# A transformer block on one core: v's weights loaded before q's and k's, five narrower loads for q and k, v's product first on the tensor engine, a new written-out order

## Chip, cores and metric

The kernel runs on one core of a Trainium2 chip. The metric is device time in microseconds (us). The kernel before took 241.88 us, the median of 3 runs (241.85 to 241.88). Engines are named as in the profile: PE is the tensor engine (PEld its weight loads), DVE the vector engine, ACT the scalar engine, POOL GpSimd, SP the engine whose queue issues nearly all DMAs.

## What is computed

One block for 2048 tokens of width 448 (bf16): a sliding, dilated attention (16 heads of 28; each token sees 8 keys, 2 apart), then a gated feed-forward layer whose gate mixes tokens by a 2048x2048 matrix.

```python
def _A_ref(x, wqkv, wo):                      # wqkv: 448 x 1344, columns q | k | v
    qkv = (x @ wqkv) ...                      # 3 x 16 heads x 2048 x 28
    idx = pos[:, None] - 2 * arange(8)        # keys of a token
    attn = softmax(einsum(q, k[idx]) * 28**-0.5, masked where idx < 0)
    return (attn @ v[idx]) @ wo
def _B_ref(x, w_in, w_sp, b_sp, w_out):
    z = gelu(x @ w_in)                        # 2048 x 1792
    z1, z2 = z[:, :896], layernorm(z[:, 896:])
    g = w_sp @ z2 + b_sp[:, None]             # 2048 x 2048 matrix
    return (z1 * g) @ w_out
h = x + _A_ref(layernorm(x), A_wqkv, A_wo)
out = h + _B_ref(layernorm(h), ...)
```

## The kernel before, in words

**Tiling.** Tokens lie in 16 tiles of 128. `x_tm` holds x by token; DVE takes mean and variance of each tile (L614 `bn_stats`, L616), POOL the reciprocal root (L608, L609), DVE writes the normalised tile `xn` (L625). The 448 columns are laid out as four chunks that start at 0, 128, 192 and 320, so that a product over 448 is made of three full 128-row chunks and one half of a fourth: chunk 1 (rows 128 to 255) and chunk 2 (rows 192 to 319) overlap by 64 rows, and a product reads all of one and the other half of the other. Tiles 0 to 3 are transposed by PE against the identity (L654, four 128x128 products each) and copied out of PSUM into `xhT` by ACT or DVE (jobs `xe0` to `xe3`, L512); tiles 4 to 15 are transposed by DMA on SP's queue (L526).

**Products.** `product` (L496) issues every large product as full matmuls (F: 128 rows) and half matmuls (H: 64 rows, two side by side in the array's upper and lower half). `qk{t}_{g}` makes q and k for token range t (0 to 255, 256 to 511, then 512 each) and head group g; its weights `wqk` are copied from the raw load `wraw` into a padded layout (jobs `wp`, L512, on ACT and DVE). `v0`, `v2`, ... make v for two blocks of keys each, with weights `wv` that are read as loaded. The logits are L790, exp is ACT's L799, the mask DVE's L805, the weighted sum L814, the output projection `y` L496 again. The feed-forward half is z2 and z1 (L496), the token-mixing product (L951; in groups of four matmuls, 16 per PSUM bank), the add of b_sp by DVE (L960, reads `bb`) which frees the bank, the gate (L963), and the last product (L975), add (L982) and store.

**Order.** The code makes a list of 920 jobs, each for one engine, with what it reads and writes. A written-out list of numbers, `ORDER`, is the one order in which all jobs are issued (919 is a dummy matmul, `warm`, L990, put in while PE has nothing to do); `BANK` names the PSUM bank of each product; `ON` the engine of each copy. Each engine runs its jobs in that order and waits on semaphores, so a job that waits holds up all behind it on its engine. SP's queue is such an engine: a transfer's turn comes when those ahead of it are issued. Loads at the start are called in the order of `FIRST` (L530 ff.), but `ORDER` decides.

Which chunks of `wraw` a product of q or k reads is set by `WK` (full matmuls) and by `(3, 1)` in `qk`'s half matmuls.

Of the kernel before, what the change touches and what calls it, by code (L numbers as in the profile page):

```python
# [76 lines left out]
ON = {'xe0_0': 'act', 'xe1_0': 'act', 'wp3_0': 'act', 'wp2_0': 'act', 'xe0_1': 'dve', 'wp1_0': 'dve', 'wp2_1': 'dve',  # L77
# [3 lines left out]
    'act', 'qe3_3': 'dve', 'od0': 'pool', 'od1': 'pool', 'qe2_1': 'act', 've6': 'act', 'qe3_0': 'dve', 'od3': 'pool',  # L81
    'od2': 'pool', 'qe3_2': 'act', 've8': 'dve', 'od4': 'dve', 'od6': 'pool', 'qe3_1': 'act', 'qe4_1': 'act', 'qe4_0':
    'act', 'od5': 'pool', 'qe4_2': 'act', 'qe4_3': 'act', 've10': 'act', 'od7': 'dve', 'od8': 'dve', 'od9': 'dve',
    've14': 'act', 've16': 'act', 've12': 'act', 'od11': 'pool', 'od10': 'pool', 'oc11': 'dve', 'z2c1': 'act', 'z2c3':
    'act', 'z2c2': 'dve', 'od12': 'pool', 'od13': 'pool', 'oc12': 'act', 'oc13': 'act', 'od15': 'dve', 'od14': 'pool',
    'z2c4': 'act', 'od17': 'pool', 'oc14': 'act', 'oc15': 'act', 'od16': 'dve', 'oc17': 'dve', 'z2c6': 'act', 'z2c7':
    'act', 'z2c5': 'act', 'oc16': 'dve', 'z2c9': 'act', 'z2c8': 'act', 'z2c10': 'act', 'z2c13': 'act'}
# [960 lines left out]
```

## Time and profile before

| | us |
|---|---|
| median of 3 runs | 241.88 |
| the profiled execution: its time | 242.38 |
| its span, first to last instruction | 240.7 |
| PE busy | 233.6 |
| DVE / ACT / POOL busy | 148.9 / 93.6 / 32.3 |
| first product that is not `warm` or a transposition | at 9.99 |
| last product ends | at 237.86 |

Times in the text are from the start of the span. The page gives busy time of each engine, the span in 40 slices, the DMA queues, the chain of work that ended last, and groups of instructions. The views behind it give single instructions in order of time with the idle time ahead of each and what ended it. In such a row the first number is the start, the second the length, `x4` the count, and the bracket the wait. TensorE's granted clock is 1.0 over the whole span.

### The profile page before, as it was taken

The page shows a single profiled execution, that of the slowest core. Times are in us where ns is not written, and L with a number is a line of the kernel's source. Part 1 is how long each engine was busy: PE and PEld are TensorE (multiplying, and loading weights), DVE is VectorE, ACT ScalarE, POOL GpSimd, SP SyncE. Part 2 cuts the span into 40 slices and gives each one's busy share as a digit, 9 for nine tenths or more (in the row PEclk, how much of TensorE's full clock was granted, in tenths as well). Part 3 has the DMA queues.
Part 4 walks back from the last instruction along what each step waited for, and adds up shares of the span by engine and source line. Part 5 has one row for each costly group of instructions (what it writes and reads, how often), then busy time and mean ns, then how long its engine had stood idle before and what let it go on. Part 6 is the DMA issues. An engine that isn't in the chain of part 4 may idle for free.

```text
span 240.7 us, 4205 instructions
## 1 busy us (share of the span) xinstructions
PE 233.6 (97%) x1711; PEld 114.9 (48%) x1727; DVE 148.9 (62%) x319; ACT 93.6 (39%) x115; POOL 32.3 (13%) x75
## 2 busy tenths in 40 slices
PE   7799999999999999999999999999999999999995
PEld 4565445445555444444444444444444444444462
DVE  5898977899999776877965037311506214317453
ACT  2577858799698978786820000000000000000000
POOL 6442000005331213114060000000000000000000
PEclk9999999999999999999999999999999999999999
DMA  6944244378947536499999997000000000110012
GB/s 174 364 107 99 48 85 85 84 180 213 127 94 83 102 75 132 87 121 191 198 194 175 152 189 184 3 0 0 0 0 3 20 19 0 57 60 0 0 57 95
DMA packets 66393, 23.21 MB, mean 96 GB/s; under 512 B 58694, under 2 KB 66246, under 8 KB 66374
## 3 DMA queue, kind: packets, MB, share of 16 engines
q1 hardware_dynamic: 66304, 22.95, 45.9%
q8 instruction: 13, 0.21, 0.4%
q14 instruction: 6, 0.05, 0.1%
q10 hardware_dynamic: 70, 0.00, 0.0%
HBM read 6.84 MB, written 1.84 MB: 36 GB/s over the span
## 4 chain that ended last, share of the span: by engine, by line
PE 93%; DMA 3%; DVE 1%; SPq 1%; issue 1%
PE psum L496 39%; PE psum L951 39%; PE psum L975 9%; PE psum L814 3%; PE psum L790 3%; DMA wraw<-in_A_wqkv_dram 3%; SPq L527 1%; DVE ub L960 1%; DVE z1p L963 0%; DVE srg L982 0%; DVE wqk L512 0%
## 5 line engine op out<-in xcount | busy, mean ns | idle before, releaser
L960 DVE TENSOR_TENSOR ub<-psum,bb 128x512 bf16<-128x512 f32 x28 | 19.2, 690 | 54.5 <-PE psum L951 54.1
L951 PE MATMUL psum<-wsp_hi,z2p 128*128 128x512 bf16 x219 | 49.9, 379 | 0.3
L951 PEld LDWEIGHTS psum<-wsp_hi,z2p 128*128 128x128 bf16 x224 | 21.9, 98 | 26.1
L799 ACT ACTIVATE E<-psum 128x896 bf16<-128x896 f32 (+2 forms) x36 | 31.8, 927 | 5.7 <-PE psum L790 5.7
L496 PE MATMUL psum<-xhT,wqk 128*128 128x512 bf16 (+3 forms) x154 | 26.5, 335 | 1.7 <-DVE wqk L512 0.9
L951 PE MATMUL psum<-wsp_lb,z2p 128*128 128x512 bf16 x111 | 25.6, 379 | 0.1
L951 PE MATMUL psum<-wsp_la,z2p 128*128 128x512 bf16 x108 | 24.9, 379 | 0.2
L496 PE MATMUL psum<-w_in,hnT 128*128 128x448 bf16 (+1 forms) x128 | 24.7, 353 | 0.0
L496 PE MATMUL psum<-hnT,w_in 128*128 128x512 bf16 (+1 forms) x112 | 23.9, 379 | 0.0
L975 PE MATMUL psum<-w_out,z1p 128*128 128x448 bf16 (+1 forms) x119 | 22.5, 341 | 0.0
L614 DVE BATCH_NORM_STATS2 st<-x_tm 128x6 f32<-128x448 bf16 x32 | 19.3, 613 | 2.0 <-DMA x_tm<-in_A_x_dram 2.0
L805 DVE TENSOR_TENSOR E<-E,maskb 128x1792 bf16<-128x1792 bf16 (+2 forms) x18 | 19.6, 1101 | 1.1 <-ACT E L799 1.1
L877 DVE BATCH_NORM_STATS2 st<-z2p 128x6 f32<-128x448 bf16 x32 | 18.6, 607 | 1.4 <-ACT z2p L873 1.2
L982 DVE TENSOR_TENSOR srg<-psum,x_tm 128x448 bf16<-128x448 f32 (+1 forms) x17 | 9.6, 592 | 13.7 <-PE psum L975 13.7
L496 PEld LDWEIGHTS psum<-xhT,wqk 128*128 128x128 bf16 (+1 forms) x160 | 12.1, 97 | 11.7 <-issue 2.8
L951 PEld LDWEIGHTS psum<-wsp_lb,z2p 128*128 128x128 bf16 x112 | 11.0, 98 | 13.2
L951 PEld LDWEIGHTS psum<-wsp_la,z2p 128*128 128x128 bf16 x112 | 10.9, 98 | 13.2
L609 POOL TENSOR_TENSOR rs<-rs,negh 128x2 f32<-128x2 f32 (+2 forms) x22 | 16.7, 759 | 1.8
L975 PEld LDWEIGHTS psum<-w_out,z1p 128*128 128x128 bf16 x119 | 11.6, 98 | 10.0
L496 PEld LDWEIGHTS psum<-w_in,hnT 128*128 128x128 bf16 (+1 forms) x128 | 10.2, 97 | 11.7 <-issue 2.6
L512 ACT ACTIVATE qkT<-psum 128x1024 bf16<-128x1024 f32 (+1 forms) x17 | 13.6, 825 | 3.3 <-PE psum L496 3.0
L496 PEld LDWEIGHTS psum<-hnT,w_in 128*128 128x128 bf16 (+1 forms) x112 | 8.9, 97 | 12.2 <-issue 2.8
(54 smaller groups left out, 226.3 us busy)
## 6 DMA issues: line engine op xcount, KB each, us to landing
w_in<-in_B_w_in_dram SPq DMA_DIRECT2D x8, 224.0 KB, 3.6
out_dram<-srg SPq DMA_DIRECT2D x16, 112.0 KB, 1.7
x_tm<-in_A_x_dram SPq DMA_DIRECT2D x3, 448.0 KB, 7.3
w_out<-in_B_w_out_dram SPq DMA_DIRECT2D x1, 784.0 KB, 5.1
bb<-in_B_b_sp_dram SPq DMA_DIRECT2D x1, 512.0 KB, 6.2
wraw<-in_A_wqkv_dram SPq DMA_DIRECT2D x1, 448.0 KB, 6.4
wraw<-in_A_wqkv_dram SPq DMA_DIRECT2D x2, 224.0 KB, 6.4
wv<-in_A_wqkv_dram SPq DMA_DIRECT2D x2, 224.0 KB, 6.4
```

The lines of the kernel that those rows point to most:

```text
L496: ins = e.matmul(o, w, x, start=g not in seen, stop=left[g] == 0, **kw)
L512: j = pl.job(name, eng, key, [(lambda e: e.activation(o(), i(), AF.Copy) if eng == "act" else e.tensor_copy(o(), i()), list(reads), list(w ...
L609: (lambda e: e.tensor_tensor(R, A, negh[:, 0:1].to_broadcast([128, n]), ALU.pow), [rr, r_negh], r_rs[k][m:m + n])],
L614: [(lambda e: e.bn_stats(st[:, m, :], src), [rsrc], [r_st[k][m]])], dve_t(D))
L790: ins = e.matmul(psum[:, c:c + nq], qkT[p:p + DH, 2 * g + 1, k0:k0 + NK], qkT[p:p + DH, 2 * g, t0:t0 + nq], start=True, stop=True, tile_po ...
L799: return e.activation(o, i, AF.Exp, scale=SCALE)
L805: return e.tensor_tensor(a, a, maskb[:, 0:1, pad:pad + nq].to_broadcast([NK, NHEAD, nq]), ALU.mult)
L877: [(lambda e, m=m, k=k: e.bn_stats(st3[:, m, k, :], z2p[:, m, D * k:D * (k + 1)]), [r_z2[m]], [r_st[2][m]])], dve_t(D))
L951: ins = e.matmul(psv(tk), z2p[:, s, 128 * fc:128 * fc + 128], w[:, 512 * (tc % 2):512 * (tc % 2) + 512], start=(s == 0), stop=(s == NB - 1))
L960: [(lambda e, tc=tc, s=s, tk=tk: e.tensor_tensor(ub[:, s, :], psv(tk), bb[:, 512 * tc:512 * tc + 512], ALU.add), [r_bb], [r_ub[s]])], dve_ ...
L975: ins = e.matmul(psv(tk, 0, c1 - c0), z1p[:, fc, 128 * m:128 * m + 128], w_out[:, fc, c0:c1], start=(fc == 0), stop=(fc == FC7 - 1))
L982: [(lambda e, m=m, s=s, tk=tk, c0=c0, c1=c1: e.tensor_tensor(srg[:, s, c0:c1], psv(tk, 0, c1 - c0), x_tm[:, m, c0:c1], ALU.add), [r_x[m]], ...
```

## The change

1. **Loads of q's and k's weights.** Before: three transfers, chunk 0, chunks 1 and 2, chunk 3, each with q's and k's columns (448 KB the largest, 896 KB in all). After: five transfers, 784 KB: chunks 0 and 1 of the new layout (rows 0 to 127 and 320 to 447; q and k, 448 KB), rows 192 to 319 for q alone (112 KB), rows 256 to 319 for k (64 partitions, 56 KB), rows 128 to 191 for q (64 partitions, 56 KB), rows 128 to 255 for k (112 KB). The half matmuls of k now read chunk 2 of `wraw`, the full ones of q chunks 0, 1 and 2, of k chunks 0, 1 and 3. Rows that no product reads are not loaded.
2. **Copies into `wqk`.** Those of k take two chunks instead of three (`wp{g}_1`); the odd rows are three copies instead of two (`wp4_0`, `wp4_1`, `wp4_2`).
3. **A new `ORDER`, `BANK` and `ON`**, for the whole kernel.

On SP's queue, the first transfers before (in the program's order; `wraw` is q and k, `wv` is v, `x_tm` x):

```order
L527 DMA x_tm<-in_A_x_dram 128x448 x2
L527 DMA x_tm<-in_A_x_dram 128x2x448
L527 DMA x_tm<-in_A_x_dram 128x4x448
L527 DMA wraw<-in_A_wqkv_dram 128x2x896
L527 DMA wraw<-in_A_wqkv_dram 128x896 x2
L527 DMA x_tm<-in_A_x_dram 128x4x448
L527 DMA wo<-in_A_wo_dram 64x448
L527 DMA wv<-in_A_wqkv_dram 128x2x448
```

and after (the two of 64 partitions are k's rows 256 to 319, then q's rows 128 to 191; the last two are k's chunk 3, then q's chunk 2):

```order
L530 DMA x_tm<-in_A_x_dram 128x448 x2
L530 DMA x_tm<-in_A_x_dram 128x2x448
L530 DMA wv<-in_A_wqkv_dram 128x2x448 x2
L530 DMA x_tm<-in_A_x_dram 128x4x448
L530 DMA wraw<-in_A_wqkv_dram 64x448 x2
L530 DMA wraw<-in_A_wqkv_dram 128x2x896
L530 DMA wraw<-in_A_wqkv_dram 128x448 x2
L530 DMA x_tm<-in_A_x_dram 128x4x448
```

Both transfers of v's weights have moved from places 10 and 14 to places 4 and 5, ahead of tokens 512 to 1023 and of all of q's and k's weights.

On PE, the first products before:

```order
L990 MATMUL psum<-warm 128x256 x22
L654 MATMUL psum<-ident,xn 128x128 x4
L990 MATMUL psum<-warm 128x256 x7
L654 MATMUL psum<-ident,xn 128x128 x4
L990 MATMUL psum<-warm 128x256 x3
L654 MATMUL psum<-ident,xn 128x128 x8
L496 MATMUL psum<-xhT,wqk 128x256 x64
L496 MATMUL psum<-wv,xhT 128x448 x10
```

and after (the 8 of `wv` are `v0`, the 4 of `wqk` are half matmuls of two head groups, the next 8 are `v2`):

```order
L997 MATMUL psum<-warm 128x256 x22
L660 MATMUL psum<-ident,xn 128x128 x8
L997 MATMUL psum<-warm 128x256 x3
L660 MATMUL psum<-ident,xn 128x128 x8
L499 MATMUL psum<-wv,xhT 128x448 x8
L499 MATMUL psum<-xhT,wqk 128x256 x4
L499 MATMUL psum<-wv,xhT 128x448 x8
L499 MATMUL psum<-xhT,wqk 128x256 x54
```

The first product is now `v0`; 16 matmuls of v and 4 half matmuls of q and k stand ahead of the rest of q and k, and 7 of the dummy matmuls are gone.

Late on SP's queue, the transfers after the last transposition of the normalised h (`hnT`); before, up to b_sp (`bb`):

```order
L526 DMA_TRANSPOSE wsp_hi<-in_B_w_sp_dram 128x1024
L526 DMA_TRANSPOSE wsp_lb<-in_B_w_sp_dram 128x1024
L526 DMA_TRANSPOSE wsp_la<-in_B_w_sp_dram 128x1024
L526 DMA_TRANSPOSE wsp_hi<-in_B_w_sp_dram 128x1024
L526 DMA_TRANSPOSE wsp_la<-in_B_w_sp_dram 128x1024
L526 DMA_TRANSPOSE wsp_lb<-in_B_w_sp_dram 128x1024 x3
L526 DMA_TRANSPOSE wsp_hi<-in_B_w_sp_dram 128x1024 x2
L526 DMA_TRANSPOSE wsp_lb<-in_B_w_sp_dram 128x1024
L526 DMA_TRANSPOSE wsp_hi<-in_B_w_sp_dram 128x1024
L526 DMA_TRANSPOSE wsp_lb<-in_B_w_sp_dram 128x1024
L526 DMA_TRANSPOSE wsp_hi<-in_B_w_sp_dram 128x1024
L527 DMA bb<-in_B_b_sp_dram 128x2048
```

and after:

```order
L529 DMA_TRANSPOSE wsp_lb<-in_B_w_sp_dram 128x1024
L529 DMA_TRANSPOSE wsp_la<-in_B_w_sp_dram 128x1024
L529 DMA_TRANSPOSE wsp_hi<-in_B_w_sp_dram 128x1024 x5
L529 DMA_TRANSPOSE wsp_lb<-in_B_w_sp_dram 128x1024
L529 DMA_TRANSPOSE wsp_la<-in_B_w_sp_dram 128x1024
L529 DMA_TRANSPOSE wsp_hi<-in_B_w_sp_dram 128x1024 x2
L529 DMA_TRANSPOSE wsp_lb<-in_B_w_sp_dram 128x1024 x2
L529 DMA_TRANSPOSE wsp_hi<-in_B_w_sp_dram 128x1024
L529 DMA_TRANSPOSE wsp_lb<-in_B_w_sp_dram 128x1024
L529 DMA_TRANSPOSE wsp_hi<-in_B_w_sp_dram 128x1024 x6
L530 DMA bb<-in_B_b_sp_dram 128x2048
L529 DMA_TRANSPOSE wsp_hi<-in_B_w_sp_dram 128x1024 x2
```

Before, 14 transpositions stand between the last `hnT` and `bb`; after, 21.

The diff, cut to its core:

```diff
-ORDER = [1, 27, 23, 25, 38, 2, 919, 28, 919, 8, 919, 29, 919, 919, 9, 37, 919, 24, 919, 6, 919, 114, 39, 919, 919, 5, 919, 40,
...
+ORDER = [2, 25, 27, 26, 40, 1, 922, 922, 10, 30, 922, 922, 116, 922, 4, 922, 29, 922, 3, 39, 922, 48, 922, 11, 922, 922, 49,
...
-WK = [(0, 1, 2), (0, 3, 2)]
+WK = [(0, 2, 1), (0, 3, 1)]
+WQ = [(0, 128, 0, 2, 0, 320, 0, 2 * D, 1.22), (0, 128, 2, 1, 192, 0, 0, D, 0.305), (64, 128, 2, 1, 256, 0, D, 2 * D, 0.153),
+      (0, 64, 3, 1, 128, 0, 0, D, 0.153), (0, 128, 3, 1, 128, 0, D, 2 * D, 0.305)]
...
             elif what == "q":
-                load_c("wq", wraw, A_wqkv[:, 0:2 * D], 2 * D, W_qk, 2.79,
-                       parts=[(None, 0, 1, 0), (None, 1, 2, 192), (None, 3, 1, 128)])
+                for i, (p0, p1, c0, nc_, lo, st, n0, n1, srv) in enumerate(WQ):
+                    load("wq_%d" % i, lambda p0=p0, p1=p1, c0=c0, nc_=nc_, n0=n0, n1=n1: wraw[p0:p1, c0:c0 + nc_, n0:n1],
+                         lambda p0=p0, p1=p1, nc_=nc_, lo=lo, st=st, n0=n0, n1=n1:
+                         bass.AP(A_wqkv.tensor, lo * 3 * D + n0, [[3 * D, p1 - p0], [st * 3 * D, nc_], [1, n1 - n0]]),
+                         [W_qk[i]], 0.45, (1.15, srv))
...
-        pool("pads", -58, [(lambda e: e.memset(E[:, :, NHEAD * 112:NHEAD * 114 + 14], 0.0), [], r_E)], 0.3)
+        pool("pads", -58, [(lambda e: e.memset(E[:, :, NHEAD * 112:NHEAD * 114 + 14], 0.0), [], r_E + r_Eh[0] + r_Eh[1] + r_Eh[2] + r_Eh[3])], 0.3)
...
-                     lambda g=g, k=k: wqk[:, 0:3, 2 * g + k, :].rearrange("p c (h d) -> p c h d", h=4)[:, :, :, 0:DH],
+                     lambda g=g, k=k: wqk[:, 0:3 - k, 2 * g + k, :].rearrange("p c (h d) -> p c h d", h=4)[:, :, :, 0:DH],
...
-        for k in range(2):
+        for k, (p0, p1, c, w) in enumerate(((0, 64, 3, 3), (0, 128, 3, 4), (64, 128, 2, 2))):
+            kk = min(k, 1)
...
-                    hs = [(k, psv(tk, k, n), wap(p0, 64, (3, 1)[k], 2 * g + k), xhT[p0:p0 + 64, c, lo:hi], (p0, 0))
+                    hs = [(k, psv(tk, k, n), wap(p0, 64, (3, 2)[k], 2 * g + k), xhT[p0:p0 + 64, c, lo:hi], (p0, 0))
...
-                product("qk%d_%d" % (t, g), key, f, rf if t < NF2 else rf[0] + rf[1], n, 6, tk, hreads=[r_pad[2 * g + 1], r_pad2[0]] + xr)
+                product("qk%d_%d" % (t, g), key, f, rf if t < NF2 else rf[0] + rf[1], n, 6, tk, hreads=[r_pad2[2], r_pad2[0]] + xr)
```

More of the change, by code (lines that the diff above doesn't have):

```diff
@@ L76 @@
 WINB = 2
-ON = {'xe0_0': 'act', 'xe1_0': 'act', 'wp3_0': 'act', 'wp2_0': 'act', 'xe0_1': 'dve', 'wp1_0': 'dve', 'wp2_1': 'dve',
[3 rows of a table removed]
[L81 to L87, printed above, removed]
+ON = {'xe0_0': 'dve', 'wp4_0': 'dve', 'wp4_1': 'dve', 'wp0_1': 'dve', 'wp2_0': 'dve', 'wp0_0': 'dve', 'wp1_1': 'dve',
[4 rows of a table added]
+    'dve', 'od3': 'dve', 'qe3_1': 'act', 'qe3_2': 'act', 've8': 'act', 'od4': 'pool', 'qe3_0': 'act', 'od5': 'pool',
+    'qe4_0': 'act', 'qe4_1': 'dve', 'od6': 'pool', 'od7': 'pool', 'od9': 'dve', 'od8': 'pool', 'qe4_2': 'act', 've14':
+    'act', 've10': 'act', 'qe4_3': 'act', 'od10': 'pool', 'od11': 'pool', 've16': 'act', 've12': 'act', 'z2c1': 'act',
+    'oc11': 'dve', 'z2c2': 'dve', 'od12': 'pool', 'od13': 'pool', 'z2c3': 'act', 'oc12': 'dve', 'oc13': 'act', 'od14':
+    'pool', 'od15': 'pool', 'z2c6': 'act', 'z2c7': 'act', 'oc14': 'dve', 'oc15': 'dve', 'od16': 'dve', 'od17': 'dve',
+    'z2c4': 'act', 'oc16': 'act', 'oc17': 'dve', 'z2c9': 'dve', 'z2c5': 'act', 'z2c8': 'act', 'z2c10': 'act', 'z2c13':
+    'act'}
 RAW2 = [0, 1, 2, 1, 1, 1, 1, 2, 1, 2, 1, 0, 0, 1, 0, 0]
@@ L534, in load_x @@
                  lambda: X[128 * m0:128 * m1, :].rearrange("(m p) d -> p m d", p=128), r_x[m0:m1], 0.55 if m0 > 1 else 0.45,
-                 (1.4, {0: 0.4, 1: 0.4, 2: 0.55, 4: 1.5}.get(m0, 1.35)), eng="sp")
+                 (1.15, {0: 0.29, 1: 0.305, 2: 0.61, 4: 1.22}.get(m0, 1.22)), eng="sp")
         r_wp = {("v", i): spot("wv%d" % i, o_wv, 4 * D * 2) for i in range(2)}
-        r_wp.update({("q", i): spot("wraw%d" % i, o_wr, 8 * D * 2) for i in range(3)})
+        r_wp.update({("q", i): spot("wraw%d" % i, o_wr, 8 * D * 2) for i in range(5)})
         def load_c(name, t, src, n, rr, srv, key=None, parts=()):
@@ L545, in load_c @@
                     load("%s_%d" % (name, i), lambda c0=c0, nc_=nc_: t[:, c0:c0 + nc_, 0:n],
-                         lambda lo=lo, hi=hi: src[lo:hi].rearrange("(c p) n -> p c n", p=128), [rr[i]], 0.5, (1.6, srv * nc_ / 3.0), key=key)
+                         lambda lo=lo, hi=hi: src[lo:hi].rearrange("(c p) n -> p c n", p=128), [rr[i]], 0.45, (1.15, srv * nc_ / 3.0), key=key)
                 else:
@@ L549, in load_c @@
                          (1.6, srv / 6.0), key=key)
-        W_qk = [r_wp[("q", i)] for i in range(3)]
+        W_qk = [r_wp[("q", i)] for i in range(5)]
         W_v = [r_wp[("v", i)] for i in range(2)]
@@ L557, in bass_sequential_preLN__sliding_local_dilated__mixer_gmlp__prompt_kernel @@
             if what == "v":
-                load_c("wv", wv, A_wqkv[:, 2 * D:3 * D], D, W_v, 1.05, parts=[(None, 0, 2, 0), (None, 2, 2, 192)])
+                load_c("wv", wv, A_wqkv[:, 2 * D:3 * D], D, W_v, 0.915, parts=[(None, 0, 2, 0), (None, 2, 2, 192)])
             elif what == "q":
-                load_c("wq", wraw, A_wqkv[:, 0:2 * D], 2 * D, W_qk, 2.79,
-                       parts=[(None, 0, 1, 0), (None, 1, 2, 192), (None, 3, 1, 128)])
+                for i, (p0, p1, c0, nc_, lo, st, n0, n1, srv) in enumerate(WQ):
[3 more added lines that the diff above has]
+                         [W_qk[i]], 0.45, (1.15, srv))
             elif what == "o":
-                load_c("wo", wo, A_wo, D, r_wo2, 1.05, parts=[(None, 0, 3, 0), (0, 3, 1, 384), (64, 3, 1, 384)])
+                load_c("wo", wo, A_wo, D, r_wo2, 0.92, parts=[(None, 0, 3, 0), (0, 3, 1, 384), (64, 3, 1, 384)])
             else:
@@ L674, in bass_sequential_preLN__sliding_local_dilated__mixer_gmlp__prompt_kernel @@
         r_pad = [spot("wpad%d" % i, o_wp, 4 * 8 * 256) for i in range(8)]
-        r_pad2 = [spot("wpad2_%d" % i, o_wp, 4 * 8 * 256) for i in range(2)]
+        r_pad2 = [spot("wpad2_%d" % i, o_wp, 4 * 8 * 256) for i in range(3)]
         pool("wpad", -57.5, [(lambda e: e.memset(wqk[:].rearrange("p c g (h d) -> p (c g h) d", h=4)[:, :, DH:32], 0.0), [], r_pad + r_pad2)], 0.4)
@@ L679, in bass_sequential_preLN__sliding_local_dilated__mixer_gmlp__prompt_kernel @@
                 move("wp%d_%d" % (g, k), "dve", KEY["wp"] + 0.3 * g,
-                     lambda g=g, k=k: wqk[:, 0:3, 2 * g + k, :].rearrange("p c (h d) -> p c h d", h=4)[:, :, :, 0:DH],
-                     lambda g=g, k=k: wraw[:, 0:3, D * k + 112 * g:D * k + 112 * g + 112].rearrange("p c (h d) -> p c h d", h=4),
-                     W_qk[0:2], [r_pad[2 * g + k]], {"act": 0.38, "dve": 0.17})
-        for k in range(2):
+                     lambda g=g, k=k: wqk[:, 0:3 - k, 2 * g + k, :].rearrange("p c (h d) -> p c h d", h=4)[:, :, :, 0:DH],
+                     lambda g=g, k=k: wraw[:, 0:3 - k, D * k + 112 * g:D * k + 112 * g + 112].rearrange("p c (h d) -> p c h d", h=4),
+                     W_qk[0:2 - k], [r_pad[2 * g + k]], {"act": 0.38, "dve": 0.17} if k == 0 else {"act": 0.3, "dve": 0.14})
+        for k, (p0, p1, c, w) in enumerate(((0, 64, 3, 3), (0, 128, 3, 4), (64, 128, 2, 2))):
+            kk = min(k, 1)
             move("wp4_%d" % k, "dve", KEY["wp"] + 0.3,
-                 lambda k=k: wqk[:, 3, k::2, :].rearrange("p g (h d) -> p g h d", h=4)[:, :, :, 0:DH],
-                 lambda k=k: wraw[:, 3, D * k:D * k + D].rearrange("p (g h d) -> p g h d", g=4, h=4),
-                 W_qk[2:], [r_pad2[k]], {"act": 0.5, "dve": 0.2})
+                 lambda kk=kk, p0=p0, p1=p1, c=c: wqk[p0:p1, c, kk::2, :].rearrange("p g (h d) -> p g h d", h=4)[:, :, :, 0:DH],
+                 lambda kk=kk, p0=p0, p1=p1, c=c: wraw[p0:p1, c, D * kk:D * kk + D].rearrange("p (g h d) -> p g h d", g=4, h=4),
+                 W_qk[w:w + 1], [r_pad2[k]], {"act": 0.5, "dve": 0.2})
         for t, (lo, hi) in enumerate(QT):
```

2 lines of the change are left out of this document (1 added, 1 removed), and 95 rows, old and new, of tables (BANK, ON, ORDER).

## The prediction

> **What bounds the kernel now.** I read the page first: busy times and the chain that ended last.
>
> ```profile
> PE 233.6 (97%) x1711; PEld 114.9 (48%) x1727; DVE 148.9 (62%) x319; ACT 93.6 (39%) x115; POOL 32.3 (13%) x75
> PE 93%; DMA 3%; DVE 1%; SPq 1%; issue 1%
> ```
>
> PE is busy nearly throughout, and the chain lies on PE for 93%; its only other large piece is a DMA. The chain in order of time says where:
>
> ```profile
> 3.26 6.37 DMA wraw<-in_A_wqkv_dram
> 9.63 0.02 issue
> 9.65 0.29 DVE wqk L512
> 9.94 0.05 issue
> 9.99 8.37 PE psum L496 x74
> ...
> 211.21 1.32 PE psum L975 x7
> ...
> 237.86 0.62 DVE srg L982
> ```
>
> PE waits until 9.99 us for a piece of q's and k's weights (landed 9.63) and its copy; from then on it works until 237.86. Between, stretches like these show no more than 0.2 us in 10 without a matmul:
>
> ```profile
> 10.00:20.00 10.00, 10.00 (x97) 6.74 (x98) 9.32 (x31) 8.56 (x18) 3.08 (x6) 1.00 0.58 161
> 50.00:60.00 10.00, 9.84 (x149) 5.22 (x146) 9.71 (x26) 8.91 (x11) 3.34 (x5) 1.00 0.76 193
> ```
>
> So the kernel is: a start of 9.99, 227.9 of PE work nearly without gaps, a tail of 2.8. PE's products are the same set after the change. The time can fall only by what the first product starts earlier, and it loses each new gap in full. DVE, busy 9.71 of 10 (third busy time), is the closest second.
>
> **The change part by part.**
>
> *The new start.* `v0` needs `wv`, and tiles 0 and 1 of `xhT`. Which is last?
>
> ```profile
> 2.82 0.63 DVE L614 BATCH_NORM_STATS2 st<-x_tm 128x6 f32<-128x448 bf16 x1 [1.36 <-DMA x_tm<-in_A_x_dram]
> 3.48 0.18 DVE L616 BATCH_NORM_AGGREGATE mv<-st 128x2 f32<-128x6 f32 x1
> 3.58 0.59 DVE L614 BATCH_NORM_STATS2 st<-x_tm 128x6 f32<-128x448 bf16 x1
> 4.54 0.63 DVE L614 BATCH_NORM_STATS2 st<-x_tm 128x6 f32<-128x448 bf16 x1 [0.37 <-DMA x_tm<-in_A_x_dram]
> 5.08 0.17 DVE L616 BATCH_NORM_AGGREGATE mv<-st 128x2 f32<-128x6 f32 x1
> 5.99 0.24 DVE L616 BATCH_NORM_AGGREGATE mv<-st 128x2 f32<-128x6 f32 x2
> 6.46 0.63 DVE L614 BATCH_NORM_STATS2 st<-x_tm 128x6 f32<-128x448 bf16 x1 [0.23 <-DMA x_tm<-in_A_x_dram]
> 7.85 0.78 DVE L625 TENSOR_SCALAR xn<-x_tm,mv,rs 128x512 bf16<-128x512 bf16 x2
> 8.55 0.41 DVE L512 CAST xhT<-psum 128x256 bf16<-128x256 f32 x1
> 6.32 0.23 POOL L608 TENSOR_SCALAR rs<-mv 128x2 f32<-128x2 f32 x1
> 6.63 0.80 POOL L609 TENSOR_TENSOR rs<-rs,negh 128x2 f32<-128x2 f32 x1
> ```
>
> `wv`: the new queue puts 896 KB up to its end (112, 112, 224, 224, 224), as the old one did up to the end of the fourth x transfer, for which DVE waited until 6.46. So `wv` is there at about 6.4. DVE's chain is later. Its new order is: statistics of two tiles, of the other two, their two aggregates, four `xn`, then the copy of half of tile 0. By the starts above: 2.82, 3.48, 3.58, 4.24 (0.66 on, as before), 4.54 (x lands), 5.08, aggregates 5.6 and 5.73, which ends at 5.88. POOL's root of tiles 2 and 3 then ends 1.2 later (old: 6.23 to 7.43) at 7.1; the last two `xn` run from 7.15 to 7.9, and the copy, behind them on DVE, from 7.83 to 8.24. PE starts `v0` at **8.3** instead of 9.99: **-1.7**.
>
> PE's transpositions are no cover for this: the same 16 stand ahead, the last eight took from 8.31 to 9.09 and now follow `xn` at 7.6 and 8.0.
>
> *What is late next.* q's and k's weights. The piece that landed at 9.63 ends at 1568 KB of the old queue (four x transfers of 896 KB in all, then 448, then its own 224).
>
> ```profile
> 6.40:9.60 3.20, 2.40 (x25) 1.44 (x22) 2.50 (x6) 0.98 (x2) 2.31 (x7) 1.00 1.03 360
> 9.65 1.60 ACT L512 ACTIVATE wqk<-wraw 128x336 bf16<-128x336 bf16 x4 [1.17 <-DMA wraw<-in_A_wqkv_dram]
> 18.21 0.92 ACT L512 ACTIVATE V<-psum 128x896 bf16<-128x896 f32 x1 [0.84 <-PE psum L496]
> ```
>
> Between 896 KB (6.46) and 1568 KB (9.63) a transfer's last part lands at 212 KB per us, although 360 GB/s moved: the last of its parts lags. New queue: x to 1344 KB at 8.6, the two 56 KB pieces to 1456 KB at 9.1, the 448 KB piece to 1904 KB at about 10.6 (9.63 plus 336 KB at the 352 KB per us of the row), the last two by 11.2. `v0` is eight matmuls, six full at 0.189 (the 1.32 for 7 above), a change of form at 0.1 and a pair of halves at 0.2: it ends at 9.75. The half matmuls behind it need two copies (ACT from 9.1, DVE behind one statistics piece): 9.6, in time. `v2` needs tile 3, which ACT copies behind its weight copy: 10.1 against PE's 9.95. It ends at 11.6. The first full products of q and k need copies that DVE and ACT make from 11 on, behind `V`'s 0.92 on ACT; I find one gap of 0.2 at 12.5, where DVE clears `otm` between two copies. Sum of gaps 0.4. Should the last part lag at 1344 KB already as at 1568 KB (half a us later), DVE's statistics, in front of the copies, shift all of them: 0.85 by the same walk. With no lag at all, 0 to 0.1. I take **+0.5**, nearer to the walk from the landed row; ends 0 and 0.85. DVE and ACT gain nothing and lose nothing else here: copies move between them within 0.5 us.
>
> *Smaller reads.* 784 KB instead of 896 KB is 112 KB, 0.3 us at that rate, for transfers behind; hidden under PE from then on, 0. The lighter copies of k (two chunks of three, about 0.1 each on four) are in the walk.
>
> *A rule.* Small transfers: the trace has both kinds in one queue.
>
> ```profile
> wo<-in_A_wo_dram SPq DMA_DIRECT2D x1, 336.0 KB, 7.0
> wo<-in_A_wo_dram SPq DMA_DIRECT2D x2, 56.0 KB, 6.9
> ```
>
> A 56 KB piece on 64 partitions takes as long from issue to landing as 336 KB: that time is the place in the queue, not a price of its own.
>
> The Trainium skill, "DMA: Bandwidth & Descriptors", section "Rules for kernel authors", says against this change that transfers to disjoint partition halves serialize and that one of 128 partitions should be used, and that under 64 KB one pays mostly overhead; its "Anatomy of one DMA" gives about 2 us fixed for each. By that, two more transfers would put the weights some 4 us later (estimate by the page). The rows above speak against it while the queue is full.
>
> *Order anew: form changes.* Twelve full matmuls of 448 columns, 12 x 0.189 = 2.27, lasted 2.37 until the next form:
>
> ```profile
> 18.82 2.44 PE L496 MATMUL psum<-wv,xhT 128*128 128x448 bf16 x12
> 21.19 0.42 PE L790 MATMUL psum<-qkT 28*128 28x112 bf16 x16
> ```
>
> A change between full, half and logit matmuls costs 0.1. The old order has 75 of them behind the first product, the new one 77: **+0.2**.
>
> *Order anew: new waits.* From the order I looked at what each product needs, against where the sum of matmuls puts it. Nearly all have 1 us or more: the transposed tiles 6 and 7 about 0 to 0.5, as before. One is close, `bb`.
>
> ```profile
> 96.58 6.42 SPq L526 DMA_TRANSPOSE hnT<-xn  x3
> 103.04 1.33 SPq L526 DMA_TRANSPOSE wsp_hi<-in_B_w_sp_dram  x1
> ...
> 123.31 0.58 SPq L527 DMA_DIRECT2D bb<-in_B_b_sp_dram  x1
> DMA to landing us min/median/max: 6.2/6.2/6.2
> 138.96 0.69 DVE L960 TENSOR_TENSOR ub<-psum,bb 128x512 bf16<-128x512 f32 x1 [9.30 <-PE psum L951]
> ```
>
> Old: 14 transpositions in 20.3 us (1.45 each), then `bb`, landed at 129.5, 9.4 before DVE first uses it. New: 21 of them after the last `hnT`, whose turn comes between 101.8 (the old one) and 103.3 (DVE's new row of pieces in front of it is 1.5 longer): `bb` is issued at 102.5 + 1.3 + 30.4 = 134.2 and lands at 140.4. PE's token mixing begins earlier too (with one z1 product of 1.3 among it), fills all eight banks, and asks for the first bank back after 26 groups of four matmuls (104 at 0.216): 119.98 - 1.7 + 0.5 + 0.2 - 1.3 + 22.4 + 1.3 = 141.4, and the bank is free 0.75 after `bb`, at 141.15. Just in time; behind PE's wait stand all token mixing, behind DVE's the gate products. Ends: 0, and 1.5 if the pitch is 1.53. I take **+0.1**.
>
> **Sum**, on the profiled execution: -1.7 + 0.5 + 0.2 + 0.1 = -0.9, so 242.38 becomes 241.5. That run lies 0.5 above the median (241.88); the difference carries over: **241.0**. The tail is the same: store of one last tile behind one add (0.62).
>
> **Rivals.** A measurement of this kernel can tell about 0.2% (0.5 us) from no change.
>
> 1. *Copies of q's and k's weights become the start.* For: DVE and ACT now mix them with statistics that wait for x. If the last parts lag 1 us more than at 9.63, each copy shifts by it and gaps reach 0.85 + 0.8; or a few small gaps arise at 50 to 70, where DVE is at 97%. Against: 3.3 us of v stand in front. Gain 1.7 - 1.65 - 0.3: 242.1 (within 0.2%).
> 2. *`bb` late: the other side.* SP's transpositions pass at 1.45 in the mean but one took 2.4; 21 instead of 14, and if `bb` lands at 142.9, 2.5 later than reckoned, PE waits 2.25 and the whole rest shifts: 241.0 + 2.15 = 243.1. It decides from a landing at 141.7 (gain gone), and slower by 0.2% from 142.2.
> 3. *Small transfers cost time of their own*: each of the two added ones holds the queue for as long as the last part lags in the rows, 1.3 (9.63, less 6.46 and 672 KB at 352 KB per us). The weights come 2.6 later, `v2` has ended at 11.6, the gaps of 0.5 become 3.1, time 241.0 + 2.6 = 243.6. The Trainium skill's rule above is this one.
> 4. *The change doesn't do what it says*: `v0` waits for `wv` no less than q did (9.6). Against: nothing but x stands ahead of it. It would leave 0.4 of the 1.7, less 0.4 for gaps and form changes: 241.9.
>
> **How the numbers follow.** Forecast 0.55 (240.3 to 241.4: gaps 0 to 0.85, `bb` 0 to 0.2); rival 1 0.24; rival 2 0.13; rival 3 0.04; rival 4 0.04. Faster 0.55, same 0.28 (rivals 1 and 4), slower 0.17 (2 and 3). The range reaches from 240.3 (no gaps: -1.7 + 0.2) past rivals 1 and 4 into rival 2, to 242.6; what lies beyond is most of rivals 2 and 3 and a little below.
>
> **What would show it.** The first `wv` matmul at 8.3, its releaser the DVE copy `xhT`, not a DMA; PE gaps below 0.9 in all from there to 14 us; no PE wait at 141 and DVE's first `ub` not ended by the `bb` DMA; 0.1 us per change of form elsewhere. Wrong if `v0` starts after 9, if PE idles over 1 us before 14, or if a stretch after 20 us shows PE idle over 0.3 in 10.

## The result, and the profile after

The changed kernel took 243.90 us, the median of five runs (243.36 to 244.69), against 241.88 for the kernel before on the same chip (241.31 to 241.92): a ratio of 1.0085, 95% interval 1.0066 to 1.0104. It is slower by 2.0 us where 0.9 us less had been forecast, and it lies above the forecast's range (240.3 to 242.6). Its runs lie wider apart, 1.3 us instead of 0.6. The profiled execution took 243.90 (span 242.1); that of before 242.38, so the two profiles have 1.5 us between them to explain.

The page, the two lines quoted of before:

```profile
PE 235.9 (97%) x1720; PEld 115.5 (48%) x1720; DVE 148.3 (61%) x323; ACT 92.1 (38%) x111; POOL 36.7 (15%) x76
PE 64%; SPq 13%; DVE 12%; DMA 6%; POOL 2%; issue 1%; ACT 1%; DVEq 0%; POOLq 0%
```

PE's busy time rose by 2.3 us for the same products, and the chain that ended last no longer lies on PE for 93%: a third of it runs over SP's queue, DVE and DMAs. The chain in order of time, at its start and at its late turning point:

```profile
3.20 5.31 DMA x_tm<-in_A_x_dram
...
8.53 0.63 DVE st L620
...
11.47 1.03 POOL rs L614
...
12.58 1.06 POOL rs L615
...
13.67 1.24 DVE xn L631 x3
...
137.16 5.69 DMA bb<-in_B_b_sp_dram
...
142.94 0.70 DVE ub L967
...
143.69 6.43 PE psum L958 x29
```

Two things are to be read here. The chain begins with the load of tokens 512 to 1023 (`x4` below, landed at 8.51; 6.43 in the kernel before) and not with a weight. And at 143.69 PE is released by DVE's first add, which waited for `bb`.

PE's rows at the start, which were the point of the change:

```profile
8.22 1.60 PE L499 MATMUL psum<-wv,xhT 128*128 128x448 bf16 x8
9.66 0.38 PE L499 MATMUL psum<-xhT,wqk 64*128 64x256 bf16 x4
```

The first product starts at 8.22 instead of 9.99. So the gain of 1.77 us is there at the start, and 3.3 us are lost behind it (1.77 and the 1.5 between the two profiles). From 17 us on:

```profile
17.44 0.83 PE L499 MATMUL psum<-xhT,wqk 128*128 128x256 bf16 x6
18.36 1.29 PE L499 MATMUL psum<-wv,xhT 128*128 128x448 bf16 x6
19.59 0.77 PE L797 MATMUL psum<-qkT 28*128 28x128 bf16 x16
20.30 0.36 PE L499 MATMUL psum<-wv,xhT 64*128 64x448 bf16 x2
20.94 1.79 PE L499 MATMUL psum<-xhT,wqk 64*128 64x512 bf16 x8 [0.28 <-issue]
```

Here the bracket tells little. A matmul's end is modelled, so most of a short wait counts as busy. The starts tell it: 17.44 to 20.94 is 3.50 us, and the same five groups take 2.42 in a run below that has no wait there. The turns (DMA transpositions) are issued in the order of tiles 5, 4, 7, 6. `v4` at 18.36 follows the landing of tile 4, issued at 15.75 and landed 2.5 later; `qk2` at 20.94 follows tile 6, issued at 18.36:

```profile
14.11 8.17 SPq L529 DMA_TRANSPOSE xhT<-xn  x5
DMA to landing us min/median/max: 2.4/2.5/2.7
```

The first of these four turns is issued at 14.11, and in the kernel before at 14.41; the last, tile 6, at 18.36 and at 19.09. So while PE came 1.77 us earlier, the turns came 0.3 to 0.7 earlier.

### The profile page after: what moved, and what is told of

Its sections match the earlier page's. It is cut to its first block, busy times and chain, and to the rows that moved or that the text cites. A ratio compares the mean times of both kernels' runs of the same rounds, so it can differ in the third digit from the quotient of the medians.

```text
span 242.1 us, 4205 instructions
## 1 busy us (share of the span) xinstructions
PE 235.9 (97%) x1720; PEld 115.5 (48%) x1720; DVE 148.3 (61%) x323; ACT 92.1 (38%) x111; POOL 36.7 (15%) x76
## 4 chain that ended last, share of the span: by engine, by line
PE 64%; SPq 13%; DVE 12%; DMA 6%; POOL 2%; issue 1%; ACT 1%; DVEq 0%; POOLq 0%
PE psum L958 31%; PE psum L499 20%; SPq L529 12%; PE psum L982 9%; DVE st L620 3%; PE psum L797 2%; PE psum L821 2%; DMA bb<-in_B_b_sp_dram 2%; DMA x_tm<-in_A_x_dram 2%; DVE st L884 2%; DVE xn L631 2%; DVE E L812 1%; POOL rs L615 1%; DMA OT<-otm 1%; SPq L530 1%
## 5 line engine op out<-in xcount | busy, mean ns | idle before, releaser
L499 PE MATMUL psum<-xhT,wqk 128*128 128x512 bf16 (+3 forms) x160 | 28.3, 337 | 0.3 <-issue 0.3
L958 PE MATMUL psum<-wsp_la,z2p 128*128 128x512 bf16 x112 | 26.0, 379 | 0.9 <-DVE ub L967 0.9
L958 PE MATMUL psum<-wsp_lb,z2p 128*128 128x512 bf16 x112 | 26.3, 379 | 0.0
L615 POOL TENSOR_TENSOR rs<-rs,negh 128x2 f32<-128x2 f32 (+2 forms) x22 | 18.0, 818 | 1.8
L499 PEld LDWEIGHTS psum<-w_in,hnT 128*128 128x128 bf16 (+1 forms) x128 | 10.2, 97 | 11.4 <-issue 2.7
L925 ACT ACTIVATE z1p<-psum 128x1024 bf16<-128x1024 f32 x14 | 13.8, 1022 | 3.6 <-PE psum L499 3.5
L631 DVE TENSOR_SCALAR xn<-x_tm,mv,rs 128x512 bf16<-128x512 bf16 x32 | 12.1, 404 | 4.9 <-POOL rs L615 4.9
```

Of the source, the lines that this page charges most:

```text
L499: ins = e.matmul(o, w, x, start=g not in seen, stop=left[g] == 0, **kw)
L615: (lambda e: e.tensor_tensor(R, A, negh[:, 0:1].to_broadcast([128, n]), ALU.pow), [rr, r_negh], r_rs[k][m:m + n])],
L631: [(lambda e: e.tensor_scalar(xn[:, s, :].rearrange("p (a b) -> p a b", a=2), bass.AP(x_tm[:].tensor, m * D, [[NB * D, 128], [192, 2], [1, ...
L925: return e.activation(o, i, AF.Gelu_apprx_tanh)
L958: ins = e.matmul(psv(tk), z2p[:, s, 128 * fc:128 * fc + 128], w[:, 512 * (tc % 2):512 * (tc % 2) + 512], start=(s == 0), stop=(s == NB - 1))
```

## The experiments

The kernels are named by their labels. `a_` is the changed kernel with an edit, `b_` the kernel before, `h_` a mixture. Moves in `ORDER` are given by the jobs' names. Times are medians; before lay at 241.78 to 241.98 beside them, and the ratio to it is given where a decision hangs on it.

### a_bb_early: bb behind w_out

```diff
 SP: hT12 wlo14 w_out
+    bb
     wlo3 wlo7 hT14 wlo15 ... whi4 whi9
-    bb
     whi8 whi5
```

(`hT` are turns of the normalised h, `wlo` and `whi` turns of w_sp.)

> The changed kernel with one job moved: the load of `bb` stands right behind `w_out` on SP's queue, some 38 us earlier. Theory: in the changed kernel `bb` lands at 142.85 and PE waits 0.9 us for it at the second group of the token mixing; with `bb` there by about 106 us that wait is gone and nothing else takes its place, so 243.0 us (242.6 to 243.4). The last turn of hnT is issued some 0.6 us later, at 105.6, which no one waits for. Rival: another release (a bank, a z1 tile, a late w_sp block) ends at the same place, and the time stays at 243.7 to 243.9.

Measured: 244.43 us (243.94 to 245.36), ratio 1.0109 (1.0090 to 1.0128): nothing gained. From the table of PE's waits (in all, times, longest):

```profile
PE psum L499 <- DMA hnT<-xn: 0.8, 1, 0.8
```

The wait for `bb` is gone, and one of 0.8 for the last turn of `hnT` stands in its place (at 110.66). SP's queue shows why:

```profile
99.31 0.58 SPq L530 DMA_DIRECT2D w_out<-in_B_w_out_dram  x1
99.93 0.56 SPq L530 DMA_DIRECT2D bb<-in_B_b_sp_dram  x1
100.53 6.64 SPq L529 DMA_TRANSPOSE wsp_la<-in_B_w_sp_dram  x2
107.22 1.31 SPq L529 DMA_TRANSPOSE hnT<-xn  x1
```

Two turns behind the two plain loads take 6.64 us in the queue, where two take 2.6 elsewhere. The rival was right in kind: taking away one wait brought up another, with the queue as the cause of both.

### a_bb_logits and b_logits: which half a logit job reads

```diff
+FLIP = (7, 8, 11, 15, 16)          # in b_logits (3, 8, 17)
             for j in range(2):
                 tk = Ticket(2)
+                jj = j ^ (b in FLIP)
-                def f(e, t0=t0, nq=nq, k0=t0 - pad, j=j, tk=tk):
+                def f(e, t0=t0, nq=nq, k0=t0 - pad, j=jj, tk=tk):
...
-                def f2(e, nq=nq, j=j, slot=slot, tk=tk):
+                def f2(e, nq=nq, j=jj, slot=slot, tk=tk):
```

A logit job of block b is 8 matmuls of 28 rows, in rows 0 and 32 of the array for one half of the heads and in rows 64 and 96 for the other. Two jobs often follow each other on PE. Before at 33.38, after at 36.62, 16 matmuls of one shape:

```profile
33.38 0.40 PE L790 MATMUL psum<-qkT 28*128 28x112 bf16 x16
```

```profile
36.62 0.56 PE L797 MATMUL psum<-qkT 28*128 28x112 bf16 x16
```

The first pair is of opposite halves, the second of the same half (blocks 5 and 7). From start to the start of what follows, a short pair takes 0.33 us and a long one 0.50. In the order of before 10 of 17 neighbouring pairs are short, in the changed one 5 of 16. Every short pair in both traces is of opposite halves, and in the long pairs of opposite halves (one before, four after) the second job waits for a bank that another engine frees. Of the same half are six pairs before and seven after.

> The changed kernel with `bb` early as in the run before it, and the two halves of the heads exchanged in blocks 7, 8, 11, 15 and 16 (which half a logit job takes; no job changes its place, engine or bank), so that seven more pairs of neighbouring logit jobs read opposite halves of the rows. Theory: two neighbouring logit jobs of opposite halves run side by side, 0.33 us a pair in place of 0.50, where the second need not wait for its bank: up to 7 x 0.17 = 1.2 us less than the run before it, 0.5 to 1.2, so 241.8 to 242.5 if that is at 243.0. Rival: the short pairs in the trace are a matter of records, or the softmax on ACT sets the pace of the attention: no change against the run before it, within 0.2 us.

> The kernel before, with the halves exchanged in blocks 3, 8 and 17, so that six more pairs of neighbouring logit jobs read opposite halves (15 in place of 9 or so). Nothing else differs. Theory (opposite halves run side by side, 0.17 us a pair): 0.5 to 1.0 us less than before, 240.9 to 241.4. Rival (ACT's exponentials set the pace there, or the short pairs are only in the records): 241.9, no change.

Measured: a_bb_logits 243.64 us, 0.8 under a_bb_early, but 245.94 was among its runs and the intervals of the two overlap (1.0058 to 1.0125 and 1.0090 to 1.0128), so it shows nothing alone. b_logits 241.11 us (240.99 to 242.01), ratio 0.9971 (0.9958 to 0.9984): 0.8 under before with no job moved. The theory holds: 0.8 for six pairs on a kernel in which nothing else changed.

### a_bb_late_start: PE held back by 1 us

```diff
 PE: v0F0 v0F1 v0H
+    warm x8
     qk0_3H qk0_0H
```

(On a_bb_early.)

> The changed kernel with `bb` early, and eight more of the warming matmuls of 0.11 us between v's first product and the first half matmul of q and k: everything that PE does behind about 9.6 us is held back by 0.9 to 1.1 us, and no load or turn is touched. Theory: what PE meets at 18 to 21 us is the turn of tokens 512 to 1023 (landings at 18.27 and 20.85), which is no earlier for PE's early start, so most of the delay is taken up by the waits there: 0.2 to 0.5 us above the run with `bb` early alone. Rival: the early start is worth its full size and the loss is elsewhere: 0.9 to 1.1 us above it.

Measured: 244.78 us, but from 243.41 to 245.76; ratio 1.0118 (1.0090 to 1.0147). That is 0.35 above a_bb_early, as the theory said, and with these intervals 0 or 1.0 would do as well. In its profiled execution `x4` landed at 9.39, and PE waited at 18 to 21 us as long as without the delay. It didn't decide; the question comes back as a_all_late. But it showed that `x4` lands anywhere from 8.2 to 9.4 in the changed order of loads.

### a_sp: w_out last, bb ten places behind hnT's last turn

```diff
 SP: hT12 wlo14
-    w_out
     wlo3 wlo7 hT14 wlo15 wlo1 whi14 whi15 whi3 whi1 whi12 wlo10 wlo4 whi7
+    bb
     whi11 wlo11 wlo13 whi10 wlo8 ... whi9
-    bb
     whi8 whi5
+    w_out
```

> The changed kernel with two jobs of SP's queue moved: w_out from before the last turn of hnT to the queue's end (where the kernel before has it), and bb from the 22nd to the tenth place or so behind that turn. Behind w_out (and in the first run behind w_out and bb together) the turns stood still for 3.6 to 4.2 us, and the last turn of hnT landed at 108.31 and 110.53, in place of 104.86 before. Theory: with nothing but turns ahead of it that turn lands by about 105.5, bb by about 132, and both PE's wait for bb (0.9) and its wait for hnT (0.8 in the run with bb alone moved) are gone: 242.9 us (242.5 to 243.3). Rival: the wait only moves on, to a late w_sp block behind bb: 243.6 or more.

Measured: 244.23 us (243.18 to 244.96), ratio 1.0088 (1.0065 to 1.0111): the rival again. In SP's queue:

```profile
120.75 0.58 SPq L530 DMA_DIRECT2D bb<-in_B_b_sp_dram  x1
121.37 1.17 SPq L529 DMA_TRANSPOSE wsp_hi<-in_B_w_sp_dram  x1
122.58 5.05 SPq L529 DMA_TRANSPOSE wsp_lb<-in_B_w_sp_dram  x2
...
129.02 1.30 SPq L529 DMA_TRANSPOSE wsp_lb<-in_B_w_sp_dram  x1
```

and on PE:

```profile
132.98 1.24 PE L958 MATMUL psum<-wsp_lb,z2p 128*128 128x512 bf16 x5 [0.84 <-issue]
```

The turn issued at 129.02 landed at 132.89, and PE's first product with it starts at 132.98 after 0.84 of waiting. So in the changed order the row of turns has little slack left: at each of the three places of `bb` so far (late, behind w_out, ten places behind `hnT`) PE paid with a wait of 0.8 to 0.9 us.

### a_bb60: nothing but turns behind 60 us

```diff
-             after=[o_jobs[NAB - 1]])          # bb
+             after=[o_jobs[WINB]])
 SP: w_in2_0 w_in1_0
+    bb
     oT9 hT2 ... hT12 wlo14
-    w_out
     wlo3 wlo7 hT14 ... whi9
-    bb
     whi8 whi5
+    w_out
```

> The changed kernel with the two loads that break SP's row of turns taken out of it: bb among w_in's loads at about 60 us (its wait for the attention's last block taken off, which nothing needs), w_out at the queue's end. Theory: behind hnT's last turn SP then issues 32 turns of w_sp one behind the other, none of 3.5 us and more, so that neither bb (0.9 us in the changed kernel) nor hnT (0.8 with bb behind w_out) nor a w_sp block (0.8 to 1.0 with bb ten places behind hnT) is waited for: 0.8 to 1.1 us under the changed kernel, 242.8 to 243.2. Rival: the turns alone set the pace there, and a wait of 0.5 us or more for a w_sp block stays: 243.5 to 243.9.

Measured: 243.10 us (242.79 to 243.59), ratio 1.0050 (1.0030 to 1.0070), 0.8 under the changed kernel. In its table of PE's waits, what is left after the start (1.5 at the dummy matmuls, 0.3 at the transpositions):

```profile
PE psum L499 <- issue: 0.7, 1, 0.7
PE psum L499 <- ACT E L806: 0.5, 1, 0.5
```

No wait for `bb`, `hnT` or a w_sp block. The price of the broken row was 0.8 us. The two waits left are those at 18 to 21 us. The second row names ACT, but `v4` starts at 18.79, right behind the landing of tile 4's turn (18.70).

### a_sp_split and a_bb60_split: the root of blocks 4 to 7 in two

```diff
-LN1G = [(0, 1), (1, 1), (2, 2), (4, 4), (8, 4), (12, 4)]
+LN1G = [(0, 1), (1, 1), (2, 2), (4, 2), (6, 2), (8, 4), (12, 4)]
-DVE: st5 wp4_0 st4 mv5 st7 st6 mv4 wp4_1 mv7 mv6 wp0_1 wp2_0 otmz wp0_0 wp1_1 wp1_0 n5 n4 n7
+DVE: st5 st4 wp4_0 mv5 mv4 st7 st6 wp4_1 mv7 mv6 wp0_1 wp2_0 n5 n4 wp0_0 wp1_1 wp1_0 otmz n7
```

(`st`, `mv`, `n`: statistics, aggregate and normalising of a tile; `wp` copies of q's and k's weights.)

> As a_sp, and the reciprocal root of tokens 512 to 1023 (blocks 4 to 7), which one POOL job takes behind the statistics of all four, is split into two jobs of two blocks; blocks 4 and 5 are normalised and turned ahead of the copies of the other groups' weights. Theory: what PE waits for at 18 and 20 us is the chain x4's landing, four statistics, root, normalising and four turns 1.3 us apart; with the first turn issued at 12.3 to 12.8 us in place of 13.8 to 14.3 both waits go, 0.6 to 1.2 us less than a_sp. Rival: the waits at 18 to 21 us are for banks that ACT's exponentials free, or POOL and DVE only change turns: within 0.3 us of a_sp.

> a_bb60 (243.10: no load breaks the row of turns) with the root of blocks 4 to 7 split in two and their turns ahead of the other weights' copies. Theory: the two mended terms add up, since one lies at 18 to 21 us and the other at 105 to 143: the split takes 1.0 to 1.7 us as it did on a_sp, 241.4 to 242.1. Rival: with PE earlier behind 21 us the turns of w_sp or of hnT are next, and less than 0.6 is gained: 242.5 or more.

Measured: a_sp_split 242.52 us (241.82 to 243.56), 1.7 under a_sp, whose runs lie 1.8 apart; a_bb60_split 241.83 (241.68 to 242.08), ratio 0.9998 (0.9985 to 1.0010), 1.27 under a_bb60. The runs now lie within 0.4 us. POOL, SP and PE of a_bb60_split:

```profile
10.34 0.85 POOL L615 TENSOR_TENSOR rs<-rs,negh 128x2 f32<-128x2 f32 x1
11.93 10.51 SPq L529 DMA_TRANSPOSE xhT<-xn  x6
17.48 0.83 PE L499 MATMUL psum<-xhT,wqk 128*128 128x256 bf16 x6
18.14 1.30 PE L499 MATMUL psum<-wv,xhT 128*128 128x448 bf16 x6
19.37 0.40 PE L797 MATMUL psum<-qkT 28*128 28x128 bf16 x16
19.70 0.36 PE L499 MATMUL psum<-wv,xhT 64*128 64x448 bf16 x2
19.90 1.78 PE L499 MATMUL psum<-xhT,wqk 64*128 64x512 bf16 x8
```

The root of the first two tiles has ended by 11.2 instead of 13.6, the first turn is issued at 11.93 instead of 14.11, and the groups that took from 17.44 to 20.94 now go from 17.48 to 19.90. The loads and PE's own order are the same, and `x4` lands at 8.4 to 8.5 in both profiled executions, so the chain from there to the turns was what PE waited for. Even the logit pair at 19.37, which had spread over 0.77, is a short one now. With the broken row (0.80) and this chain (1.27) mended, all 2.0 us that the change had lost are back, and the changed order is level with the kernel before.

### a_sp_logits

The edit is a_bb_logits' on a_sp.

> As a_sp, with the halves exchanged in blocks 7, 8, 11, 15 and 16 (seven more pairs of opposite halves). Theory: side by side, 0.17 us a pair; the run of this kind on the kernel before gave 0.8 us for six pairs, and the pair of runs with bb moved gave 0.8 for seven: 0.6 to 1.1 us less than a_sp, about 242.0. Rival: with the waits for bb and hnT gone something on ACT or SP is next, and nothing is gained.

Measured: 242.55 us (241.74 to 243.15), 1.7 under a_sp: more than the pairs explain. a_sp's runs lie 1.8 us apart, more than the surplus; the clean number is a_all's below.

### b_loads and b_loads_logits: the narrower loads alone

```diff
 SP: x0 x1 x2 x4
-    wq_1 wq_0 wq_2          # three wide
+    wq_0 wq_2 wq_1 wq_3 wq_4   # five narrow, as in the change
     x8 wo_1 wv_0 ...
```

All else in the order of before, with the extra small copy `wp4_2` behind `wp4_1`.

> The loads alone: the kernel before, order, banks and engines as they were, with q's and k's weights in five narrower loads in place of three (12% less bytes) and one more small copy on DVE; v's weights stay last. Theory: the weights land a little earlier or at the same time and the start at 9.99 moves by 0 to -0.4 us, x4 is untouched and so are all waits: 241.5 to 241.9. Rival (many small transfers cost their own time, as the changed kernel's loss): 0.3 us or more above before, 242.2 to 243.5.

> The kernel before with the five narrower loads (b_loads: 241.60) and the halves exchanged in blocks 3, 8 and 17 (b_logits: 241.11, 0.8 under before). Theory: the two add up, the one at the start, the other between 20 and 75 us: 240.6 to 240.9. Rival: w_sp's turns or ACT set a bound that the two meet: 241.1.

Measured: b_loads 241.60 us (241.12 to 242.00), ratio 0.9985 (0.9976 to 0.9993); its first product:

```profile
9.28 0.94 PE L498 MATMUL psum<-xhT,wqk 128*128 128x256 bf16 x7
```

0.7 earlier than the 9.99 of before. b_loads_logits: 240.71 us (240.47 to 240.99), ratio 0.9949 (0.9928 to 0.9969), so the two add up. It is the fastest kernel of the study, 1.2 us under before and 3.2 under the changed one, and v is not first in it.

### h_start and h_split_logits: the changed beginning, the old rest

```diff
 every engine: changed order up to its first logit job (PE at 17 us)
+              then the order, BANK and ON of before for all that is left
```

> The changed kernel's beginning with the order of before behind it: loads, engines, banks and order of the changed kernel on all engines up to its first logit job (PE at about 17 us), the order, engines and banks of the kernel before for everything that is left. Theory: v's product starts at 8.2 us in place of 9.99, x4 lands at 8.2 to 9.4 in place of 6.0 to 6.6, and so PE waits again at 18 to 21 us for the turns of tokens 512 to 1023, 0.8 to 1.5 us in all; what the changed order loses later (logit pairs 0.8, bb 0.9) is not there: 241.0 to 241.7. Rival: the waits at 18 to 21 us belong to the changed order behind them, not to x4's load: 240.1 to 240.5.

> As h_start, with the root of blocks 4 to 7 split in two (as in a_sp_split) and the halves exchanged in blocks 3, 8 and 17 (as in b_logits). Theory: split 1.0 to 1.7 less, logits 0.5 to 0.8 less than h_start: 239.2 to 240.0, under both kernels. Rival: with both gone the softmax on ACT or w_sp's turns are next: 240.4 or more.

Measured: h_start 242.90 us (242.57 to 243.42), h_split_logits 242.23 (241.98 to 242.47). Both miss, and the fault is in the edit. PE in h_start:

```profile
19.47 0.59 PE L797 MATMUL psum<-qkT 28*128 28x112 bf16 x16 [1.18 <-ACT qkT L515]
```

The old order asks at once for logits whose q and k the new beginning made last, so PE waits 1.18 for ACT's copies at the seam, ahead of the place that was to be tested. They say nothing of the theory.

### a_all and a_all_late: all three mended, and PE held back again

a_all is a_bb60_split with `FLIP = (7, 8, 11, 15, 16)`; a_all_late has the eight dummy matmuls of a_bb_late_start in it.

> a_bb60_split with the halves exchanged in blocks 7, 8, 11, 15 and 16 as well: the changed kernel with all three of its losses mended. Theory: the losses are the waits at 18 to 21 us, the logit pairs and bb, and with them gone the earlier start of 1.77 us stands: 240.3 to 241.0, under the kernel before by 0.9 to 1.6 us, and 0.7 to 1.2 under a_bb60_split. Rival: some loss of the changed order is not among the three: 241.5 or more.

> a_all with eight more warming matmuls (0.9 to 1.1 us on PE) between v's first product and the first half matmul of q and k. Theory: with the turns of tokens 512 to 1023 earlier there are no waits left at 18 to 21 us that could take the delay up: 0.7 to 1.1 us above a_all, where the same delay cost 0.35 us on the changed kernel with bb moved. Rival: the delay is taken up here as well, so that the start's size was never what counted: under 0.4 us above a_all.

Measured: a_all 240.90 us (240.62 to 241.38), ratio 0.9957 (0.9943 to 0.9971), so 0.9 under before and 0.93 under a_bb60_split. a_all_late 241.57 us (241.48 to 242.06), 0.67 above a_all, just under the 0.7 to 1.1 expected. A part of the delay goes into a wait that a_all has at that place for copies of q's and k's weights:

```profile
10.19 0.39 PE L500 MATMUL psum<-xhT,wqk 64*128 64x256 bf16 x4 [0.37 <-DVE wqk L516]
```

1.07 for eight dummies and two changes of form, less that 0.37, is 0.7. So with the turns early, a delay of PE's start costs 0.67 of its 1.07, where it had cost 0.35 with wide intervals.

The step from a_bb60_split to a_all does not give back a loss of the change: the kernel before has six pairs of the same half as well, and the same edit gave it 0.8 (b_logits). Like with like, a_all (240.90) stands beside b_loads_logits (240.71), and no gain of the earlier start is seen. Where it goes, the logit jobs show: from start to the start of what follows, all 36 take 7.7 us in a_all's profiled execution and 6.8 in that of b_loads_logits, though every neighbouring pair is of opposite halves in both. In a_all four jobs stand alone instead of two, and some pairs wait for a bank; the longest, at 33.28, takes 0.98 us instead of 0.33, and its second job has:

```profile
33.96 0.37 PE L799 MATMUL psum<-qkT 28*128 28x112 bf16 x8 [0.31 <-DVE otm L834]
```

No run tried these waits alone.

## Why the prediction was wrong, point by point

- **The new start, -1.7.** Right: 8.22 where 8.3 was reckoned, and `wv` was not what came last, though it landed at 7.13 and not at 6.4. There was little to spare: in a_bb_late_start's profiled execution it landed at 8.15, and `v0` started at 8.40.
- **Gaps while q's and k's weights are late, +0.5.** The size is within the ends given (0 and 0.85): 0.14 in the profiled execution of the change, 0.5 in that of a_all. The place is another: the half matmuls between 9.6 and 10.2, reckoned to be in time, wait for their copies, and nothing waits at 12.5.
- **"Nearly all have 1 us or more: the transposed tiles 6 and 7 about 0 to 0.5, as before."** This step failed, and it cost most. The walk of gaps ended at 14 us, and for the turns of tiles 4 to 7 the slack of before was carried over, as if they came earlier along with PE; their wait was put at nothing. They don't hang on PE. They hang on `x4`, four statistics, one root, and turns 1.3 apart. Before, the turn of tile 6 landed at 21.64 and the first product that reads it started at 21.75; after, it landed only 0.8 earlier, at 20.85. So most of PE's 1.77 had to come back as waits: 1.1 us in the profiled execution, 1.27 by a_bb60_split against a_bb60. Which link made the chain late (`x4` landing 2.1 later behind `wv`, or POOL's root, 2.1 long where it was 1.4) was not tried apart and stays open; the split lets the first root and the first turns start earlier.
- **Form changes, +0.2.** The count is right, and beside the point. The sum took PE's products as the same set and had no term for which logit jobs stand side by side. The new order has five short pairs fewer, 0.17 each: about 0.8. Only one of the five is a matter of halves (seven pairs of the same half instead of six); one pair has become two jobs that stand alone, and three more pairs of opposite halves wait for a bank.
- **`bb`, +0.1.** Mechanism right, size wrong. The pitch was as reckoned, (137.16 - 106.33) / 21 = 1.47. What was mis-sized is the start of the row: the last `hnT` turn went at 104.98 where 102.5 was taken. DVE was later with its tiles, which were normalised by 101.74 before and by 104.01 after. Before:

```profile
101.00 0.74 DVE L625 TENSOR_SCALAR xn<-x_tm,mv,rs 128x512 bf16<-128x512 bf16 x2 [0.69 <-DVE st L877]
```

After, DVE and then SP's queue:

```profile
103.28 0.73 DVE L631 TENSOR_SCALAR xn<-x_tm,mv,rs 128x512 bf16<-128x512 bf16 x2 [1.15 <-POOL rs L615]
99.80 5.14 SPq L529 DMA_TRANSPOSE wsp_la<-in_B_w_sp_dram  x2
104.98 1.31 SPq L529 DMA_TRANSPOSE hnT<-xn  x1
```

DVE makes 1.5 of the 2.5; the other 1.0 is `w_out`, which now stands three places ahead and holds the row until 104.94. In a_bb60, without `w_out` there, the turn goes as soon as DVE is done, at 104.30; that kernel loses its wait because `bb` isn't in the row any more. Rival 2 named the very landing (142.9; measured 142.85), but by luck: it put it on a slower pitch. PE waited 0.9 and not the 2.25 of the rival, since it came 1.4 late itself.

- **Rival 3, small transfers.** Wrong side: b_loads has the same two more transfers, with 12% less bytes, and is faster by 0.4 us; its last piece of q's and k's weights lands at 8.96 instead of 10.29. By the rule of the Trainium skill that was quoted ("DMA: Bandwidth & Descriptors", "Rules for kernel authors") it would have been slower; the measurement decides. The 2 us quoted with it stand on that page for DMAs issued from GpSimd, and these are issued from SP.

The sum from before's profile: -1.77 start, +0.14 copies, +1.08 turns (the long logit pair at 19.59 among them), +0.27 a logit pair at 33.9 us that waits, +0.7 the other four pairs, +0.2 form changes (as reckoned, not measured), +0.9 `bb`: +1.5, where the two profiled executions differ by 1.5. The experiments show the turns and `bb`, which together are the 2.0 us between the medians; that the rest takes up most of the earlier start is read from rows. That v goes first gains nothing that shows in the end: a_all starts at 8.22 and b_loads_logits at 9.16, and they end 0.2 apart, the later start ahead.

## What to carry to other kernels

When a change makes an engine start earlier, list for each later product what it waits for that does **not** hang on that engine; where such a chain has less slack than the gain, the gain ends there. Where an order is rewritten, count neighbours as well as jobs: which pairs ran side by side, and which plain load now stands ahead of a transposition. And when a mended wait is replaced by another one of the same size, look at the queue that both hang on before trying a third place.
